# An attention backward pass: x^T and g^T of block 2 from staged tiles by TensorE, block 1 started tile by tile, K^T in five buffers ordered six steps ahead, dV in four

## Chip, cores and metric

One core of one Trainium2 chip. The metric is the device time of one launch in microseconds (us), the median of several executions.

## The reference

Two independent attention blocks (A, here "block 1", and B, "block 2") with a key and value cache, outputs concatenated, and the gradient of everything:

```python
# per block: B=8, Sq=96, D=640, H=32, Sk=512, Dh=128, bf16
def block(x, k_cache, v_cache, wq, wo):
    q = (x @ wq).reshape(B, Sq, H, Dh).transpose(0, 2, 1, 3)
    scores = einsum("bhqd,bhkd->bhqk", q, k_cache) * Dh ** -0.5
    p = softmax(scores)
    o = einsum("bhqk,bhkd->bhqd", p, v_cache)
    return o.transpose(0, 2, 1, 3).reshape(B, Sq, H * Dh) @ wo

out   = concatenate([block(A...), block(B...)], axis=-1)
grads = vjp(out, all ten inputs)(grad_out)      # returned with out: 11 outputs
```

## The kernel before

Work is put into steps ("ticks"): every piece is added with a step and a slot in it, and at the end all pieces are emitted sorted by step and slot. One step is one (head, batch) pair, 3.1 us at the steady pace; heads go in pairs (HP = 2), so K, V, K^T, V^T, dK, dV move once for two steps. All DMAs are issued by one engine's queue (SP) in the order in which they are added (`sp(...)` chains them). The parts that matter here, cut (`...`):

```python
OFF = dict(kt=-1, vt=2, vn=1, kn=4, dv=7, dk=10, s2=3, s3=3, s4=4, s5=5, s6=6, s7=8, s8=9)   # steps after the pair's own
HP = 2
HK = [   # head 0 and head 1 of a pair: steps of its projections (p..) and of its weight gradients (q..)
    dict(pA=-10, pB=-7, pC0=[-6, -4], pC1=[-5, -3], pD1=-2, pD0=0, qA0=21, qA1=25, qB=[28, 25]),
    dict(pA=-7, pB=-2, pC0=[-1, 1], pC1=[0, 2], pD1=3, pD0=6, qA0=29, qA1=33, qB=[36, 33], qD=[...]),
]

    def setup_T(which_, c):                        # x^T or g^T, column chunk c
        def f():
            ...
            if not first:                          # block 2: a transposing DMA from DRAM
                sp(nc.sync.dma_start_transpose(S[key][:, c, :], src_flat[:, c * 128:(c + 1) * 128]))
                return
            pt = bank([128, TT * 128], BF16, "tp_ps")
            for t in range(TT):                    # block 1: TensorE, six tiles of 128 tokens
                nc.tensor.transpose(pt[:, t * 128:(t + 1) * 128], S["x_nat" if which_ == 0 else "g_nat"][:, t, ...], ident[:])
            evac("act" if c % 2 == 0 else "dve", S[key][:, c, :], pt[:])
        return f

    if first:
        em.add(tick0 - 14, SL_LOAD, setup_nat(0))  # all of x, then all of g, 960 KB each
        em.add(tick0 - 14, SL_LOAD, setup_nat(1))
        ...
    else:
        for i in range(2 * DC):                    # ten transposing DMAs, 13 to 7 steps before block 2 begins
            em.add(tick0 - 13 + (2 * i) // 3, SL_LOAD + 0.5, setup_T(i // DC, i % DC))
        em.add(tick0 + 22, SL_LOAD + 0.5, setup_nat(1))
        em.add(tick0 + 25, SL_LOAD + 0.5, setup_nat(0))

    def p_ldT(h, b, which):                        # K^T or V^T of a pair of heads
            t_ = kvp.tile([128, F4 * KC, 16], BF16, name=key + "_p", bufs=4)
            sp(nc.sync.dma_start_transpose(t_[:], src))
    def c_s4(h, b):                                # dV of one (head, batch)
            ...
            if j == 0:
                st["dV_p"] = wk.tile([128, HP, KC * 128], BF16, name="dV_sb", bufs=3)
            nc.scalar.activation(dV_p[:, j], dV_ps[:], ACT.Identity, scale=1.0)
    def qB(h, di):                                 # dwo of one head, in two pieces (512 and 128 columns)
            if "dwo_sb" not in st:
                st["dwo_sb"] = hd.tile([128, D], BF16, name="dwo_sb", bufs=1)
            ...
            evac(EV["qB%d" % di], dwo_sb[:, c0:c0 + w], w_ps[:])       # ACT
    ...
            for di in range(len(dsplits)):
                em.add(c0t + hk["qB"][di], SL_HEAD + 1, qB(h, di))
            em.add(c0t + max(hk["qB"]) + 2, SL_LOAD + 0.3, qB_st(h))   # the store of dwo
```

Of the kernel before, what the change touches and what calls it, by code (L numbers as in the profile page):

```python
# [15 lines left out]
class Emitter:  # L16
# [24 lines left out]
SL_GRP = 95  # L41
SL_SETUP = 96

OFF = dict(kt=-1, vt=2, vn=1, kn=4, dv=7, dk=10, s2=3, s3=3, s4=4, s5=5, s6=6, s7=8, s8=9)
HP = 2
HK = [
    dict(pA=-10, pB=-7, pC0=[-6, -4], pC1=[-5, -3], pD1=-2, pD0=0, qA0=21, qA1=25, qB=[28, 25]),
    dict(pA=-7, pB=-2, pC0=[-1, 1], pC1=[0, 2], pD1=3, pD0=6, qA0=29, qA1=33, qB=[36, 33], qD=[(37, 0, 2), (38, 2, 4), (39, 4, 5)]),
]
EV = dict(pB0="act", pB1="dve", pC00="act", pC01="act", pC10="act", pC11="dve", pD0="dve", pD1="dve", qA0="dve", qA1="dve", qB0="act", qB1="act", qD="dve", gU="act")  # L50
GSPREAD0 = 9
PRIO_OFF = 2000
# [19 lines left out]
def build_block(tc, em, tick0, blk, x, kc, vc, wq, wo, g_all, out_all, dx, dk, dv, dwq, dwo, ident, ones, pools, HG=4, first=True, groups=None):  # L72
# [42 lines left out]
    S = {}  # L115
# [3 lines left out]

    sp = pools["sp"]  # L120

    def setup_T(which_, c):
        def f():
            key = "xT" if which_ == 0 else "gT"
            if c == 0:
                S[key] = const.tile([128, DC, T], BF16, name=key, bufs=1)
            src_flat = x_flat if which_ == 0 else g_flat
            if not first:
                sp(nc.sync.dma_start_transpose(S[key][:, c, :], src_flat[:, c * 128:(c + 1) * 128]))
                return  # L130
            pt = bank([128, TT * 128], BF16, "tp_ps")
            for t in range(TT):
                nc.tensor.transpose(pt[:, t * 128:(t + 1) * 128], S["x_nat" if which_ == 0 else "g_nat"][:, t, c * 128:(c + 1) * 128], ident[:])
            evac("act" if c % 2 == 0 else "dve", S[key][:, c, :], pt[:])
        return f

    def setup_nat(which_):
        def f():
            key = "x_nat" if which_ == 0 else "g_nat"
            src_flat = x_flat if which_ == 0 else g_flat  # L140
            t_ = const.tile([128, TT, D], BF16, name=key, bufs=1)
            sp(nc.sync.dma_start(t_[:], src_flat.rearrange("(t p) d -> p t d", p=128)))
            S[key] = t_
        return f

    def setup_acc():
# [11 lines left out]
                nc.vector.tensor_scalar(dst, src, float(sc), None, op0=ALU.mult)  # L158

    if first:  # L160
        em.add(tick0 - 14, SL_LOAD, setup_nat(0))
        em.add(tick0 - 14, SL_LOAD, setup_nat(1))
        for c in range(DC):
            em.add(tick0 - 9, SL_SETUP, setup_T(0, c))
            em.add(tick0 - 8, SL_SETUP, setup_T(1, c))
    else:
        for i in range(2 * DC):
            em.add(tick0 - 13 + (2 * i) // 3, SL_LOAD + 0.5, setup_T(i // DC, i % DC))
        em.add(tick0 + 22, SL_LOAD + 0.5, setup_nat(1))
        em.add(tick0 + 25, SL_LOAD + 0.5, setup_nat(0))  # L170

    def pA(h):
        def f():
            g, hh = h // HG, h % HG
            if hh == 0:
                G[g] = dict(wo_r=grp.tile([128, HG, D], BF16, name="wo_r", bufs=2))
            wo_h = G[g]["wo_r"][:, hh]
            sp(nc.sync.dma_start(wo_h, wo[h * 128:(h + 1) * 128, :]))
            j = h % HP
            if j == 0:  # L180
                wq_p = hd.tile([128, DC, HP * 128], BF16, name="wq_p", bufs=2)
                with nc.allow_non_contiguous_dma(reason="per-pair wq slice"):
                    sp(nc.sync.dma_start(wq_p[:], wq_v[:, :, h * 128:(h + HP) * 128]))
            else:
                wq_p = HS[(blk, h - j)]["wq_p"]
            HS[(blk, h)] = dict(wo_h=wo_h, wq_p=wq_p, wq_h=wq_p[:, :, j * 128:(j + 1) * 128])
        return f

    def pB(h):
        def f():  # L190
            st = HS[(blk, h)]
            woT_ps = bank([128, DC * 128], BF16, "woT_ps")
            for c in range(DC):
                nc.tensor.transpose(woT_ps[:, c * 128:(c + 1) * 128], st["wo_h"][:, c * 128:(c + 1) * 128], ident[:])
            woT_h = hd.tile([128, DC * 128], BF16, name="woT_h", bufs=1)
            evac(EV["pB0"], woT_h[:], woT_ps[:])
            st["woT_h"] = woT_h
            wqT_ps = bank([128, DC * 128], BF16, "wqT_ps")
            for c in range(DC):
                nc.tensor.transpose(wqT_ps[:, c * 128:(c + 1) * 128], st["wq_h"][:, c, :], ident[:])  # L200
            wqT_h = hst.tile([128, D], BF16, name="wqT_h")
            evac(EV["pB1"], wqT_h[:], wqT_ps[:])
            st["wqT_h"] = wqT_h
            st["QT_h"] = hd.tile([128, T], BF16, name="QT_h", bufs=4)
            st["dOT_h"] = hd.tile([128, T], BF16, name="dOT_h", bufs=4)
        return f

    def pC(h, which, si):
        def f():
            st = HS[(blk, h)]  # L210
            (t0, w) = tsplits[si]
            if which == 0:
                dst = st["QT_h"]
                lhs = lambda c: st["wq_h"][:, c, :]
                rhsT = S["xT"]
                sc = scale
            else:
                dst = st["dOT_h"]
                lhs = lambda c: st["woT_h"][:, c * 128:(c + 1) * 128]
                rhsT = S["gT"]  # L220
                sc = None
            q_ps = bank([128, w], F32, "q_ps")
            for c in range(DC):
                nc.tensor.matmul(q_ps[:], lhs(c), rhsT[:, c, t0:t0 + w], start=(c == 0), stop=(c == DC - 1))  # L224
            evac(EV["pC%d%d" % (which, si)], dst[:, t0:t0 + w], q_ps[:], sc)
        return f
# [19 lines left out]
    def p_ldT(h, b, which):  # L246
        def f():
            key = "KT" if which == 0 else "VT"
            t_ = kvp.tile([128, F4 * KC, 16], BF16, name=key + "_p", bufs=4)
            src = (kc if which == 0 else vc)[b, h:h + HP].rearrange("h (r f) d -> (h r) (f d)", r=R8)  # L250
            sp(nc.sync.dma_start_transpose(t_[:], src))
            for j in range(HP):
                half = t_[:, :, j * R8:(j + 1) * R8]
                CS.setdefault((blk, h + j, b), {})[key] = half.rearrange("p (f c) r -> p f c r", c=KC)
        return f
# [38 lines left out]
    def c_s2b(h, b):  # L294
        def f():
            with tc.high_priority(PRIO_OFF):
                st = CS[(blk, h, b)]
                E_sb = wk.tile([Sq, Sk], BF16, name="E_sb", bufs=2)
                rowsum = wk.tile([Sq, 1], F32, name="rowsum", bufs=3)
                nc.scalar.activation(E_sb[:].rearrange("q (a f) -> q a f", f=F4), st["S_ps"][:].rearrange("q (f a) -> q a f", f=F4), ACT.Exp, bias=st["negm"][:], scale=1.0, accum_out=rowsum[:])  # L300
                st["E_sb"], st["rowsum"] = E_sb, rowsum
                del st["S_ps"]
        return f
# [19 lines left out]
    def c_s45(k5, k4, k6):  # L323
        def f():
# [17 lines left out]
                    nc.tensor.transpose(PT_ps[:, c * Sq:(c + 1) * Sq], P_sb[:, c * 128:(c + 1) * 128], ident[0:Sq, 0:Sq])  # L342
            if ot_view is not None:
                OT_ps, hs, tok = ot_view
                nc.vector.tensor_copy(hs["OT_h"][:, tok], OT_ps)  # L345
            if k4 is not None:
                PT_sb = wk.tile([128, KC * Sq], BF16, name="PT_sb", bufs=3)
                nc.scalar.activation(PT_sb[:], PT_ps, ACT.Identity, scale=1.0)  # L348
# [3 lines left out]
    def c_s4(h, b):  # L352
        def f():
            st = CS[(blk, h, b)]
            hs = HS[(blk, h)]
            P_sb = st["P_sb"]
            dV_ps = bank([128, KC * 128], F32, "dV_ps")
            for c in range(KC):
                nc.tensor.matmul(dV_ps[:, c * 128:(c + 1) * 128], P_sb[:, c * 128:(c + 1) * 128], hs["dOnat_h"][:, b * 128:(b + 1) * 128], start=True, stop=True)  # L359
            j = h % HP  # L360
            if j == 0:
                st["dV_p"] = wk.tile([128, HP, KC * 128], BF16, name="dV_sb", bufs=3)
            dV_p = CS[(blk, h - j, b)]["dV_p"]
            nc.scalar.activation(dV_p[:, j], dV_ps[:], ACT.Identity, scale=1.0)  # L364
        return f
# [164 lines left out]
    for g in range(NG):  # L530
        h0 = GH0[g]
        for hh in range(groups[g]):
            h = h0 + hh
            j = h % HP
            c0t = tick0 + (h - j) * B
            hk = HK[j]
            em.add(c0t + (hk["pA"] if h > 0 or not first else -15), SL_LOAD, pA(h))
            em.add(c0t + hk["pB"], SL_HEAD, pB(h))
            em.add(c0t + OFF["s5"], SL_LOAD, h_alloc(h))
            for si in range(NTS):  # L540
# [4 lines left out]
            for b in range(B):  # L545
                ct = c0t + b * HP + j
                if j == 0:
                    em.add(ct + OFF["kt"], SLOTS["LOAD"], p_ldT(h, b, 0))
                    em.add(ct + OFF["vt"], SLOTS["LOAD"], p_ldT(h, b, 1))
                    em.add(ct + OFF["vn"], SLOTS["LOAD"] + 0.1, p_ldn(h, b, 1))  # L550
                    em.add(ct + OFF["kn"], SLOTS["LOAD"] + 0.1, p_ldn(h, b, 0))
                    em.add(ct + OFF["dv"], SLOTS["LOAD"] + 0.2, p_st(h, b, 1))
                    em.add(ct + OFF["dk"], SLOTS["LOAD"] + 0.2, p_st(h, b, 0))
# [156 lines left out]
```

## Time and profile before

| | kernel before |
|---|---|
| time, median of 3 (range) | 1689.2 us (1685.68 to 1693.71) |
| profiled execution | 1677.57 us, its span 1675.8 us, mean clock 0.995 |
| PE idle in the whole span (sum of gaps between matmuls) | 63.4 us |
| four heads at the steady pace (32 S matmuls) | 100.0 us |

The profiled execution of before is a quick one: 10 us under its median. How to read the stretches: cut where every 32nd S matmul begins (four heads of work); a group that takes 100 us runs at PE's own pace, and what it takes beyond 100 is lost somewhere.

### The profile page before, as it was taken

How to read it: one execution, taken by the hardware profiler on the slowest of the kernel's cores; microseconds unless marked ns; L12 is line 12 of the kernel's file. 1: busy time of each engine (PE TensorE's matmuls, PEld its weight loads, DVE VectorE, ACT ScalarE, POOL GpSimd, SP SyncE). 2: the span in 40 equal slices, each digit the busy share in tenths (PEclk: the TensorE clock that was granted, in tenths of full speed). 3: DMA queues.
4: the chain of work that ended last, by engine and by line, in shares of the span. 5: the costliest groups of instructions: out<-in, count | busy, mean ns of one | idle time of the engine just before them, and what ended most of it. 6: DMA issues, size and time to landing. Idle time of an engine off the chain costs nothing.

```text
span 1675.8 us, 55270 instructions
## 1 busy us (share of the span) xinstructions
PE 1609.0 (96%) x20670; PEld 1263.1 (75%) x20860; DVE 1363.4 (81%) x3381; ACT 1334.4 (80%) x3511; POOL 535.2 (32%) x1030
## 2 busy tenths in 40 slices
PE   6999999999999999999799999999999999999998
PEld 5777777777777777777577777777787777777776
DVE  4876788888888888888588778888888888888886
ACT  6988877878787797887677789788787877878783
POOL 2333333333333232332233323333233333333231
PEclk9999999999999999999899999999999999999999
DMA  8999999999999999999999999999999999999996
GB/s 242 265 272 262 258 275 292 267 287 271 277 281 269 264 294 287 272 280 256 262 297 288 270 290 286 278 292 277 295 267 270 275 286 278 271 276 259 277 277 192
DMA packets 378381, 458.11 MB, mean 273 GB/s; under 512 B 44288, under 2 KB 369920, under 8 KB 369920
## 3 DMA queue, kind: packets, MB, share of 16 engines
q1 hardware_dynamic: 378112, 454.57, 103.0%
q8 instruction: 163, 2.67, 0.7%
q14 instruction: 106, 0.87, 0.1%
HBM read 159.12 MB, written 159.12 MB: 190 GB/s over the span
## 4 chain that ended last, share of the span: by engine, by line
PE 73%; ACT 8%; DMA 8%; DVE 6%; issue 4%; SPq 1%; POOL 0%; ACTq 0%; DVEq 0%; POOLq 0%
PE q_ps L224 11%; PE o_ps L508 10%; PE dwo_ps L463 6%; PE dwq_ps L483 5%; PE S_ps L288 5%; PE dV_ps L359 5%; PE dP_ps L383 5%; PE dK_ps L425 5%; PE optp_ps L335 4%; PE optp_ps L342 4%; PE dq_dst_ps L409 4%; PE dq_dst_ps L402 4%; DMA out_dram<-dV_sb 3%; PE n_ps L239 3%; ACT E_sb L300 3%
## 5 line engine op out<-in xcount | busy, mean ns | idle before, releaser
L319 POOL TENSOR_SCALAR P_sb<-E_sb,rinv 96x512 bf16<-96x512 bf16 x512 | 353.9, 691 | 328.8 <-DVE rinv L310 327.9
L430 ACT ACTIVATE dK_sb<-dK_ps 128x512 bf16<-128x512 f32 x512 | 304.9, 595 | 168.7 <-PE dK_ps L425 158.8
L373 POOL TENSOR_TENSOR prod<-OT_h,dOT_h 128x96 bf16<-128x96 bf16 x512 | 187.4, 366 | 780.7 <-DVE OT_h L345 764.5
L387 DVE SCALAR_TENSOR_TENSOR dS_sb<-dP_ps,dl_ps,P_sb 96x512 bf16<-96x512 f32 x512 | 382.2, 746 | 28.4 <-PE dl_ps L385 17.5
L300 ACT ACTIVATE E_sb<-S_ps,negm 96x512 bf16<-96x512 f32 x512 | 349.7, 683 | 69.7 <-DVE negm L290 64.3
L290 DVE TENSOR_REDUCE negm<-S_ps 96x1 f32<-96x512 f32 x512 | 347.2, 678 | 57.9 <-PE S_ps L288 57.1
L364 ACT ACTIVATE dV_sb<-dV_ps 128x512 bf16<-128x512 f32 x512 | 309.6, 605 | 34.9 <-DMA out_dram<-dV_sb 23.9
L348 ACT ACTIVATE PT_sb<-optp_ps 128x384 bf16<-128x384 bf16 x512 | 253.5, 495 | 0.7 <-PE optp_ps L342 0.5
L411 DVE COPY dST_sb<-dq_dst_ps 128x384 bf16<-128x384 bf16 x512 | 177.8, 347 | 35.9 <-PE dq_dst_ps L409 30.9
L288 PE MATMUL S_ps<-KT_p,QT_h 128*96 128x512 bf16 x512 | 194.2, 379 | 8.6 <-DMA KT_p<-in_A_k_cache_dram 4.3
L425 PE MATMUL dK_ps<-Qnat_h,dS_sb 96*128 96x128 bf16 x2048 | 198.6, 220 | 0.0
L359 PE MATMUL dV_ps<-dOnat_h,P_sb 96*128 96x128 bf16 x2048 | 198.5, 219 | 0.2 <-ACT dV_sb L364 0.2
L383 PE MATMUL dP_ps<-VT_p,dOT_h 128*96 128x512 bf16 x512 | 195.5, 382 | 1.2 <-DMA VT_p<-in_B_v_cache_dram 0.9
L335 PE MATMUL optp_ps<-PT_sb,V_sb 128*128 128x96 bf16 x2048 | 172.4, 206 | 10.5 <-ACT PT_sb L348 5.4
L402 PEld LDWEIGHTS <-K_sb 128*128 128x128 bf16 x2048 | 133.6, 98 | 56.5 <-issue 7.0
L342 PE MATMUL optp_ps<-ident,P_sb 96*128 96x96 bf16 x2048 | 172.1, 205 | 3.7 <-POOL P_sb L319 3.7
L409 PE MATMUL dq_dst_ps<-ident,dS_sb 96*128 96x96 bf16 x2048 | 172.5, 206 | 0.0
L402 PE MATMUL dq_dst_ps<-dST_sb,K_sb 128*128 128x96 bf16 x2048 | 171.3, 206 | 0.0
L345 DVE CAST OT_h<-optp_ps 128x96 bf16<-128x96 f32 x512 | 126.4, 247 | 32.8 <-PE optp_ps L342 30.1
L508 PE MATMUL o_ps<-wo_r,OT_h 128*128 128x128 bf16 (+1 forms) x721 | 144.3, 294 | 2.5
L508 PE MATMUL o_ps<-wqT_h,dQT_h 128*128 128x128 bf16 (+1 forms) x721 | 144.2, 294 | 2.5
L224 PE MATMUL q_ps<-gT,woT_h 128*128 128x512 bf16 (+1 forms) x624 | 135.0, 324 | 8.5 <-DMA gT<-in_grad_out_dram 7.3
(66 smaller groups left out, 3019.4 us busy)
## 6 DMA issues: line engine op xcount, KB each, us to landing
out_dram<-dV_sb SPq DMA_DIRECT2D x256, 256.0 KB, 4.7
out_dram<-dK_sb SPq DMA_DIRECT2D x256, 256.0 KB, 4.7
V_sb<-in_A_v_cache_dram SPq DMA_DIRECT2D x128, 256.0 KB, 4.7
K_sb<-in_A_k_cache_dram SPq DMA_DIRECT2D x128, 256.0 KB, 4.5
V_sb<-in_B_v_cache_dram SPq DMA_DIRECT2D x128, 256.0 KB, 4.6
K_sb<-in_B_k_cache_dram SPq DMA_DIRECT2D x128, 256.0 KB, 4.5
out_dram<-dwo_sb SPq DMA_DIRECT2D x64, 160.0 KB, 4.6
out_dram<-dwq_sb SPq DMA_DIRECT2D x32, 320.0 KB, 4.7
```

The costliest lines, as they stand in the source:

```text
L224: nc.tensor.matmul(q_ps[:], lhs(c), rhsT[:, c, t0:t0 + w], start=(c == 0), stop=(c == DC - 1))
L290: nc.vector.tensor_reduce(negm[:], S_ps[:], axis=AX.X, op=ALU.max, negate=True)
L300: nc.scalar.activation(E_sb[:].rearrange("q (a f) -> q a f", f=F4), st["S_ps"][:].rearrange("q (f a) -> q a f", f=F4), ACT.Exp, bias=st["n ...
L319: nc.gpsimd.tensor_scalar(P_sb[:], st["E_sb"][:], st["rinv"][:], 0.0, op0=ALU.mult, op1=ALU.add)
L359: nc.tensor.matmul(dV_ps[:, c * 128:(c + 1) * 128], P_sb[:, c * 128:(c + 1) * 128], hs["dOnat_h"][:, b * 128:(b + 1) * 128], start=True, s ...
L364: nc.scalar.activation(dV_p[:, j], dV_ps[:], ACT.Identity, scale=1.0)
L383: nc.tensor.matmul(dP_ps[:], hs["dOT_h"][:, tok], st["VT"], start=True, stop=True)
L387: nc.vector.scalar_tensor_tensor(dS_sb[:].rearrange("q (a f) -> q a f", f=F4), dP_ps[:].rearrange("q (f a) -> q a f", f=F4), dl_ps[:, 0:1] ...
L402: nc.tensor.matmul(dQT_ps, st["K_sb"][:, c, :], st["dST_sb"][:, c * Sq:(c + 1) * Sq], start=(c == 0), stop=(c == KC - 1))
L425: nc.tensor.matmul(dK_ps[:, c * 128:(c + 1) * 128], dS_sb[:, c * 128:(c + 1) * 128], hs["Qnat_h"][:, b * 128:(b + 1) * 128], start=True, s ...
L430: nc.scalar.activation(dK_p[:, j], dK_ps[:], ACT.Identity, scale=1.0)
L508: nc.tensor.matmul(o_ps[:], src[:, t * 128:(t + 1) * 128], rhs, start=(hh == 0), stop=(hh == groups[g] - 1))
```

## The change

Intent: ten transposing DMAs at the crossing from block 1 to block 2 are replaced by twelve plain tile loads and 60 TensorE transposes; block 1 begins on single x tiles as they land; K^T is ordered two steps earlier with a fifth buffer, so that a late load does not stop PE; dV gets a fourth buffer, so that ACT does not wait for stores. Besides, g and x for block 2's weight gradients are loaded in twelve pieces instead of two, and therefore the first dwo work of block 2 moves later (`HK2`).

```diff
-OFF = dict(kt=-1, vt=2, vn=1, ...)
+OFF = dict(kt=-3, vt=2, vn=1, ...)
+HK1 = [dict(HK[0], pB=2, pC0=[-8, -6], pC1=[3, 3], pD1=3.5, pD0=6), dict(HK[1], pB=2, pC0=[-8, -6], pC1=[3, 3.6], pD1=4, pD0=7)]
+HK2 = [dict(HK[0], qA0=29, qB=[32, 31]), dict(HK[1], qA0=33)]
+GT0, ST0, ST1, NG0, NX0 = 2, -14, 7, 21, 26
...
+    def setup_stage(which_, t):                   # one tile of 128 tokens into a staging buffer
+            S[(key, t)] = wk.tile([128, D], BF16, name="ob", bufs=3)
+            sp(nc.sync.dma_start(S[(key, t)][:], src_flat[t * 128:(t + 1) * 128, :]))
-    def setup_T(which_, c):
+    def setup_T(which_, t):                       # five transposes of one tile, one evacuation
+            src = S[nat][:, t, :] if first else S.pop((nat, t))[:]
+            pt = bank([128, DC * 128], BF16, "tp_ps")
+            for c in range(DC):
+                nc.tensor.transpose(pt[:, c * 128:(c + 1) * 128], src[:, c * 128:(c + 1) * 128], ident[:])
...
     if first:
-        em.add(tick0 - 14, SL_LOAD, setup_nat(0))
-        em.add(tick0 - 14, SL_LOAD, setup_nat(1))
+        for t in range(TT):                       # x tile by tile, g later
+            em.add(tick0 - 15, SL_LOAD + (2 if late else 0), setup_nat(0, t, t + 1))
+            em.add(tick0 - (7 if late else 9), SL_HEAD, setup_T(0, t))
+            em.add(tick0 + GT0, SL_LOAD - 2, setup_nat(1, t, t + 1))
+            em.add(tick0 + GT0, SL_HEAD + (2 if late else -1), setup_T(1, t))
     else:
-        for i in range(2 * DC):
-            em.add(tick0 - 13 + (2 * i) // 3, SL_LOAD + 0.5, setup_T(i // DC, i % DC))
-        em.add(tick0 + 22, SL_LOAD + 0.5, setup_nat(1))
-        em.add(tick0 + 25, SL_LOAD + 0.5, setup_nat(0))
+        for i in range(2 * TT):
+            em.add(tick0 + ST0 + (ST1 * i) // (2 * TT), SL_LOAD + 0.5, setup_stage(i // TT, i % TT))
+            em.add(tick0 + ST0 + (ST1 * i) // (2 * TT) + 2, SL_SETUP, setup_T(i // TT, i % TT))
+        for t in range(TT):
+            em.add(tick0 + NG0 + t, SL_LOAD + 0.5, setup_nat(1, t, t + 1))
+            em.add(tick0 + NX0 + (3 * t) // 2, SL_LOAD + 0.5, setup_nat(0, t, t + 1))
...
-            t_ = kvp.tile([128, F4 * KC, 16], BF16, name=key + "_p", bufs=4)
+            t_ = kvp.tile([128, F4 * KC, 16], BF16, name=key + "_p", bufs=5 if which == 0 else 4)
...
-                st["dV_p"] = wk.tile([128, HP, KC * 128], BF16, name="dV_sb", bufs=3)
+                st["dV_p"] = wk.tile([128, HP, KC * 128], BF16, name="dV_sb", bufs=4)
...
-            hk = HK[j]
+            hk = (HK if h >= HP else HK1 if first else HK2)[j]
```

Cut from the diff: the load of wq as a piece of its own, rowsum in two buffers instead of three, and a higher priority for the evacuation of O^T.

## The prediction

> **What bounds the kernel now.** I read the page first, then the stretches, the waits, the timeline of the queue that issues all DMAs, and raw DMA packet records.
>
> ```profile
> span 1675.8 us, 55270 instructions
> PE 1609.0 (96%) x20670; PEld 1263.1 (75%) x20860; DVE 1363.4 (81%) x3381; ACT 1334.4 (80%) x3511; POOL 535.2 (32%) x1030
> ...
> q1 hardware_dynamic: 378112, 454.57, 103.0%
> ```
>
> PE looks like the bound, but the DMA engines are as full: packet time equals 103% of 16 engines' span. The stretches say where PE loses. I cut at every 32nd S matmul (four heads; here rounded) after finding their times in the timeline.
>
> ```profile
> core 0: us, PE busy (x) PEld busy (x) DVE busy (x) ACT busy (x) POOL busy (x), PEclk, DMA share, GB/s
> 0.00:20.00 20.00, 11.59 (x121) 9.34 (x124) 4.41 (x10) 9.11 (x13) 0.70 (x6) 1.00 0.92 250
> 20.00:105.00 85.00, 74.99 (x1010) 58.86 (x1014) 67.68 (x171) 75.27 (x199) 31.92 (x61) 1.00 1.01 260
> 105.00:210.00 105.00, 101.49 (x1286) 78.78 (x1297) 77.81 (x189) 88.94 (x238) 33.32 (x64) 1.00 1.04 261
> ...
> 717.00:833.00 116.00, 102.95 (x1285) 80.27 (x1296) 85.56 (x213) 82.11 (x215) 32.93 (x63) 0.94 1.03 259
> 833.00:939.00 106.00, 101.96 (x1291) 79.88 (x1301) 86.12 (x215) 81.79 (x217) 33.54 (x65) 0.98 1.06 288
> ...
> 1041.00:1541.00 500.00, 494.58 (x6439) 390.85 (x6498) 429.11 (x1070) 409.08 (x1081) 166.80 (x320) 1.00 1.05 278
> ```
>
> The row from 1041 to 1541 is five groups of four heads at 100 us each, 1 us of PE idle per group: PE's own pace. Against 100, the group that crosses from block 1 to block 2 (717 to 833) loses 16, the next one 6, the one from 105 to 210 about 5, the others of block 1 together some 6. The first 105 us lose 18.4 us of idle PE (20 less 11.59, 85 less 74.99).
>
> ```profile
> PE tp_ps L133 <- DMA x_nat<-in_A_x_dram: 8.0, 1, 8.0
> PE q_ps L224 <- DMA gT<-in_grad_out_dram: 7.3, 2, 5.3
> ...
> ACT dV_sb L364 <- DMA out_dram<-dV_sb: 23.9, 24, 2.6
> ```
>
> The big waits are all for DMAs: x at the start, g^T at the crossing, the buffers of dV (ACT's wait, which reaches PE only when ACT falls behind). Now the issuing queue at the crossing:
>
> ```profile
> 783.36 4.21 SPq L129 DMA_TRANSPOSE xT<-in_B_x_dram  x2
> 787.67 1.46 SPq L251 DMA_TRANSPOSE VT_p<-in_A_v_cache_dram  x1
> 789.18 0.58 SPq L178 DMA_DIRECT2D wo_r<-in_B_wo_dram  x1
> 789.80 0.43 SPq L183 DMA_DIRECT2D wq_p<-in_B_wq_dram  x1
> ...
> 793.53 1.56 SPq L251 DMA_TRANSPOSE KT_p<-in_A_k_cache_dram  x1
> ...
> 796.27 3.53 SPq L129 DMA_TRANSPOSE gT<-in_grad_out_dram  x2
> ```
>
> Each row starts where the one before ends. I checked this for the whole run: the 1766 DMA issues take 1490.6 us and the gaps between them 162 us (median 46 ns); from 28 us to 1642 us no gap exceeds 0.45 us. Nor is the queue waiting for buffers: when a K^T load is issued, the last reader of the buffer it overwrites has been done for 8 to 18 us (means of eight loads in a row, after the first eight). So the DMA stream runs without rest at nearly PE's pace. From the end of a K^T issue to its use there are only 6 to 12 us on average, 3 to 4 us at the narrowest, and the load itself takes 5.2 us to land. That is the reading on which I choose the number: **PE and the DMA stream are co-bounds**, and before 939 us it is the stream that sets the pace.
>
> **What the Trainium skill says.** "Perfetto Trace Analysis", section "What DMA-bound means", names a sequencer track that is solid DMA slices as one form of DMA-bound, and notes that such a slice is descriptor generation, not movement. The trace agrees on the solid track. "VectorE: DVE Perf Modes", section "The three transpose paths", gives 390 ns for a 128x128 transpose on TensorE and 1309 ns by DMA. Here the 30 g transposes take 1.84 us together, 61 ns each when queued, and an x^T transposing DMA (six such blocks) occupies the issuing queue 1.3 us or more. "Advanced Engine Details and Errata", section "X-Bar Transpose (TRN2)", calls transposing DMAs as fast as regular ones. The packets disagree for x^T and g^T: 256-byte packets of 34.9 ns against 61.3 ns for 1280-byte ones, 2.8 times the time per byte. "TensorE: Matmul & The Clock Gate", Part 1, says the clock halves after an idle window of about 3.4 us; PEclk is 0.68 in 800 to 820 us, around the 5.29 us wait for g^T.
>
> **The change part by part.**
>
> *Crossing.* Ten transposing DMAs go: 16.15 us of the issuing queue and 7680 packets x 34.9 ns / 16 engines = 16.7 us of all engines. Twelve tile loads of 160 KB come: 12 x (0.53 + 0.09) = 7.4 us of queue and 12 x 128 packets x 61.3 ns / 16 = 5.9 us of engines. Net 9 us of queue, 11 us of engine time. Six K^T steps there took 53.2 us (770.43 to 823.59) for a usual 37.5, so 15.7 extra; with the new loads I expect 6 or 7 extra. PE gets 60 transposes x 61 ns = 3.7 us, and ACT and DVE six evacuations each (ACT 0.8, DVE 0.56 by the rows of x^T before), which have room at 80%. Since PE waited 12 us there, its 3.7 us lie mostly in what would be waiting. Gain: 16 less about 6, so **10**, of which some 1.5 is the restored clock.
>
> *x and g of block 2 for the weight gradients* are loaded in twelve pieces over ticks 21 to 33, not as two of 960 KB. The bytes are the same, and the stretch 833 to 939 already moves 288 GB/s, the most of any; the K^T issue just behind g_nat took 4.72 us. Spreading removes such clumps, the load stays: **2** of the 6.
>
> *Start.* Four x tiles, then wq, then the rest; PE can begin near 3.5 us (an estimate: a 160 KB load lands in 3 to 4 us, first issue 0.74) instead of 8.0. Q^T comes before g, so the first S moves from 21.4 to about 12. But K^T for the 17th pair step is issued at 99 and used at 105: by then the DMA stream paces. What the stream gains is its one real rest, 3.8 us from 24.4 to 28.2, where the first dV store waited for dV, and somewhat fuller engines (0.76 of their time in 20 to 30 us). Gain **5**, not the 9 that PE's idle time suggests.
>
> *dV in four buffers* removes most of ACT's 23.9 us; of the PE stalls only those behind ACT gain (1.46 us at 71.8, about 1 us each at 518, 925, 944). *K^T two ticks earlier and a fifth buffer*: in an unbroken stream this only moves K^T ahead of other loads. V is next in need, with about the same margin (6.4 us, lands in 4.7), so PE's 15.5 us of K^T waits (4.3 on PE, 11.2 on its weight loads, overlapping) shrink by little before V takes their place. Together **3**.
>
> *Rest.* OT_h first on DVE, rowsum in two (E_sb has two already), the later first dwo of block 2: 0. The tail after the last S (1638.9) is untouched.
>
> Sum: 10 + 2 + 5 + 3 = 20, and the rate after 1041 is PE's own. I take 2 off again for new order waits (second rival): 18 of 1676, 1.1%.
>
> **Rivals.**
>
> *PE is the only bound.* Then nearly all excess is there to be had: start 9 to 11, crossing 11, the stretch behind it 4, K^T and dV waits 6: 30 to 35 us, about 1656. For it: PE 96%, flat 100 us groups. Against it: the unbroken queue and the 3 to 4 us minimum margins.
>
> *The staged tiles block the queue.* They have three buffers, tiles are ordered 7/12 tick apart and transposed two ticks later, so the fourth load waits for PE's first transposes; a waiting load holds up K^T and V behind it. With a tick of 3.1 us this could cost 3 to 6 us at the crossing, most of the gain: about 1675. For it: the queue trails PE's order by about a tick already. Against: K^T's two extra ticks cover it.
>
> *Only PE's wait moves.* Loads that start earlier find full engines and land later; V or wo becomes the wait in place of K^T and g^T: gain under 8, 1682 or more.
>
> **Range and chances.** 1689.2 - 18 x (1689.2 / 1675.8) = 1671; I lean towards the first rival by a quarter of the difference and say **1667**. The range 1654 to 1681 spans from the first rival to the third. Faster by 2% needs below 1655.4, nearly all of the first rival: 0.15. Slower needs a blocked queue all along: 0.03. Within 2%: 0.82.
>
> **What would show it.** Right: L133 with 120 transposes, no L129; first S near 12 us; no rest of the queue near 25 us; the group across the crossing near 106 and PEclk 1.0 there; dV waits under 5 us; the issuing queue still solid; the five late groups still 100. Wrong if the first 105 us shorten by 9 or more, or groups of block 1 all fall to 100 (then PE alone was the bound), or if the queue shows waits at L133's tiles (then the second rival).

## More of the kernel before

Runs were made on more than one chip, and the same kernel differs between chips by more than most effects studied here; so times are compared only within one set, a set being kernels that ran on the same chip together with the kernel before.

## The result, and the profile after

| | before | after |
|---|---|---|
| median (range, runs) | 1687.79 us (1685.68 to 1693.71, 4) | 1670.28 us (1666.86 to 1672.68, 4) |
| profiled span, clock | 1675.8 us, 0.995 | 1668.0 us, 0.993 |
| PE idle in the span | 63.4 us | 47.5 us |

The ratio is 0.9889, 95% interval 0.9858 to 0.9921: within 2%. Here and below a ratio is the mean time of one kernel's runs over the mean of the other's of the same rounds, so not quite the ratio of the medians quoted. The gain is 17.5 us by the medians. The changed kernel was run again in two later sets on chip 5: 13.5 us (ratio 0.9942) and 17.1 us (0.9889) below the kernel before.

The page after, first line, engines and the DMA queue:

```profile
span 1668.0 us, 55517 instructions
PE 1616.8 (97%) x20920; PEld 1265.7 (76%) x20920; DVE 1368.3 (82%) x3389; ACT 1339.2 (80%) x3517; POOL 533.5 (32%) x1030
...
q1 hardware_dynamic: 372160, 454.57, 102.7%
```

Both bounds are as full as they were: the DMA engines moved the same 454.57 MB in 5952 fewer packets, and their share went from 103.0% to 102.7%.

The stretches after, cut at its own 32nd S matmuls (columns: stretch, length, busy time and count of PE, weight loads, DVE, ACT and POOL; the last three are clock, DMA share and GB/s):

```profile
0.00:20.00 20.00, 13.07 (x114) 8.74 (x115) 5.14 (x12) 9.60 (x16) 1.20 (x7) 1.00 0.88 224
20.00:105.00 85.00, 77.72 (x1049) 62.45 (x1047) 69.01 (x173) 75.23 (x198) 32.06 (x62) 0.96 1.03 272
...
708.00:819.00 111.00, 105.69 (x1365) 83.00 (x1364) 88.81 (x223) 86.69 (x226) 33.60 (x65) 0.98 1.02 263
819.00:927.00 108.00, 101.91 (x1301) 79.30 (x1300) 86.17 (x215) 82.45 (x216) 33.22 (x65) 0.98 1.05 288
927.00:1038.00 111.00, 100.75 (x1299) 79.29 (x1298) 78.07 (x189) 89.56 (x239) 33.13 (x64) 0.95 1.03 274
1041.00:1541.00 500.00, 498.02 (x6518) 391.33 (x6516) 430.59 (x1072) 410.75 (x1084) 167.07 (x322) 1.00 1.05 279
```

The row 927 to 1038 is the surprise: 10 us of idle PE and a clock of 0.95 in a group which in the kernel before took 101.9 us. The row 20 to 105 has a clock of 0.96, where the kernel before had 1.00. From the starts of S matmuls 0, 32, 224, 256, 288, 320 and 480, the stages of both profiles:

| stage (S matmuls) | before | after | gain |
|---|---|---|---|
| start to 32 | 104.8 | 103.5 | 1.3 |
| 32 to 224, block 1 | 611.8 | 604.8 | 7.0 |
| 224 to 256, the crossing | 116.6 | 110.5 | 6.1 |
| 256 to 288 | 106.1 | 108.2 | -2.1 |
| 288 to 320 | 101.9 | 111.4 | -9.5 |
| 320 to 480 | 500.3 | 499.3 | 1.0 |
| 480 to the end | 134.3 | 130.3 | 4.0 |

The sum is 7.8 us, the difference of the spans; the 10 us more that the medians show cannot be laid to stages, because before was profiled in one quick run only. The 4.0 us of the last row belong to no term of the prediction, which held the end untouched. In before PE waits there for ACT (1.2, 0.7 and 0.3 us between 1547 and 1552 us), and after it does not; no run tells which part of the change removed that. One profile each is also little: the changed kernel was profiled three times, and its crossing took 110.5, 105.9 and 111.1 us.

The waits after (time in all, times, longest):

```profile
ACT dwo_sb L162 <- DMA out_dram<-dwo_sb: 13.9, 5, 10.1
...
PE optp_ps L350 <- ACT dwo_sb L162: 9.8, 1, 9.8
...
PE woT_ps L209 <- DMA wo_r<-in_A_wo_dram: 4.8, 4, 2.2
...
PE optp_ps L350 <- DMA V_sb<-in_B_v_cache_dram: 4.2, 2, 2.6
...
PE tp_ps L151 <- DMA ob<-in_grad_out_dram: 3.3, 2, 2.8
```

The waits for g^T, for K^T and for the buffers of dV are gone from the top. In their place stands one wait of ACT for the store of dwo, 10.1 us long, and PE's wait for ACT, 9.8 us. In place of g^T PE waits for the staged tiles (3.3 us for g, 1.8 for x), and in place of K^T for wo (4.8 us in four places, 0.3 before) and for V (4.2 us in two). V was predicted; wo stands only in the third rival. In the group of dV's evacuations (busy us, mean ns | idle before, releaser; the row before ended "34.9 <-DMA out_dram<-dV_sb 23.9") nothing is left:

```profile
L380 ACT ACTIVATE dV_sb<-dV_ps 128x512 bf16<-128x512 f32 x512 | 309.7, 605 | 0.3 <-PE dV_ps L375 0.3
```

The timeline of the stall (start, duration; in brackets the idle time ahead of it and its releaser), ACT and the issuing queue:

```profile
927.25 0.49 ACT L364 ACTIVATE PT_sb<-optp_ps 128x384 bf16<-128x384 bf16 x1
937.79 0.28 ACT L162 ACTIVATE dwo_sb<-dwo_ps 128x128 bf16<-128x128 f32 x1 [10.05 <-DMA out_dram<-dwo_sb]
```

```profile
933.31 0.46 SPq L485 DMA_DIRECT2D out_dram<-dwo_sb  x1
```

ACT stands from 927.74 to 937.79 before the 128-column piece of head 1's dwo. It may overwrite the one `dwo_sb` only when head 0's dwo has been stored, and that store is issued at 933.31, and ACT goes on 4.5 us later. The steps say why. `HK2` puts head 0's pieces at steps 32 and 31, so its store, two steps after the later of its two pieces, comes at step 34; head 1's first piece stays at step 33. Before, the store was at step 30. A wait of one instruction stops everything behind it on its engine: the Trainium skill, "Perfetto Trace Analysis", section "Per-instruction lifecycle: what the profiler-reported window actually captures", calls ACT, DVE and GPSIMD strict FIFOs, and the trace agrees, for the 0.59 us evacuation of dV behind it starts only at 937.96.

The stall costs more than PE's 9.8 us of waiting. PE goes on at 938.12, and the clock stays low for some time after:

```profile
938.00:941.20 3.20, 3.08 (x27) 2.64 (x27) 1.78 (x5) 2.69 (x8) 1.03 (x2) 0.50 1.07 351
```

It is 0.50 from 931.0 to 941.2 us. A matmul of dP, 0.38 us long just before the stall, takes 0.63 us in that row. Half of the 3.1 us is 1.5 us (an estimate from the clock of 0.50); with the wait that is 11.3 of the 11.6 us by which this group exceeds 99.8.

The crossing in the issuing queue (a row with x2 is two issues in a row, from the start of the first to the end of the second):

```profile
771.49 4.69 SPq L140 DMA_DIRECT2D ob<-in_B_x_dram  x2
776.23 1.10 SPq L266 DMA_TRANSPOSE KT_p<-in_A_k_cache_dram  x1
777.39 0.57 SPq L277 DMA_DIRECT2D V_sb<-in_A_v_cache_dram  x1
778.05 0.41 SPq L286 DMA_DIRECT2D out_dram<-dV_sb  x1
```

Two tile loads of some 0.4 us each span 4.69 us: between them the queue stood 3.94 us. The second issue starts at 775.84, as PE's transposes of an earlier tile end at 775.81, so it waited for a staging buffer; K^T, V and dV stood behind. The Trainium skill, "DMA: Bandwidth & Descriptors", section "Anatomy of one DMA — SWDGE (gpsimd) path", says that DMA engines do not wait on semaphores, a wait being served on the issuing sequencer before dispatch. The trace shows just that, on the path that SP uses. This is the second rival of the prediction. In again_after the same wait took 5.13 us. What it costs in the time no run shows.

### The profile page after: what moved, and what is told of

Its sections match the earlier page's. It is cut to its first block, busy times and chain, and to the rows that moved or that the text cites. A ratio compares the mean times of both kernels' runs of the same rounds, so it can differ in the third digit from the quotient of the medians. Undisturbed runs are those within 1.5% of the kernel's fastest.

```text
span 1668.0 us, 55517 instructions
## 1 busy us (share of the span) xinstructions
PE 1616.8 (97%) x20920; PEld 1265.7 (76%) x20920; DVE 1368.3 (82%) x3389; ACT 1339.2 (80%) x3517; POOL 533.5 (32%) x1030
## 3 DMA queue, kind: packets, MB, share of 16 engines
q1 hardware_dynamic: 372160, 454.57, 102.7%
## 4 chain that ended last, share of the span: by engine, by line
PE 79%; ACT 6%; DMA 6%; DVE 5%; issue 2%; SPq 1%; POOL 0%; ACTq 0%; DVEq 0%
PE q_ps L239 11%; PE o_ps L524 10%; PE dwo_ps L479 6%; PE dV_ps L375 5%; PE dP_ps L399 5%; PE dwq_ps L499 5%; PE S_ps L303 5%; PE dK_ps L441 5%; PE optp_ps L350 4%; PE optp_ps L357 4%; PE dq_dst_ps L418 4%; PE dq_dst_ps L425 4%; PE n_ps L254 3%; PE nat_ps L465 2%; DVE negm L305 2%
## 5 line engine op out<-in xcount | busy, mean ns | idle before, releaser
L350 PE MATMUL optp_ps<-PT_sb,V_sb 128*128 128x96 bf16 x2048 | 172.4, 206 | 18.7 <-ACT dwo_sb L162 9.8
L524 PE MATMUL o_ps<-wo_r,OT_h 128*128 128x512 bf16 (+1 forms) x768 | 149.3, 299 | 0.0
L524 PE MATMUL o_ps<-wqT_h,dQT_h 128*128 128x512 bf16 (+1 forms) x768 | 148.5, 299 | 0.0
L350 PEld LDWEIGHTS <-V_sb 128*128 128x128 bf16 x2048 | 125.2, 97 | 23.0 <-issue 18.2
```

Source lines behind the costliest of these rows:

```text
L350: nc.tensor.matmul(OT_ps, st["V_sb"][:, c, :], st["PT_sb"][:, c * Sq:(c + 1) * Sq], start=(c == 0), stop=(c == KC - 1))
L524: nc.tensor.matmul(o_ps[:], src[:, t * 128:(t + 1) * 128], rhs, start=(hh == 0), stop=(hh == groups[g] - 1))
```

## The experiments

Twelve runs, three sets. Time before on the same chip in the same set: 1683.22 us in the first (1670.34 to 1690.88, 11 runs, chip 5), 1665.55 in the second (1658.78 to 1669.52, 11 runs, chip 15), 1687.79 in the third (1679.79 to 1698.83, 11 runs, chip 5 again). On chip 15 the kernel before is about 20 us faster. In the set of chip 15 the changed kernel was not run, and the kernel before was not profiled. Groups of four heads are quoted from the profiles as three numbers: 224 to 256 (the crossing), 256 to 288, and 288 to 320.

| run | chip | median (range) | ratio to before [95%] | groups |
|---|---|---|---|---|
| again_after | 5 | 1669.72 (1667.38 to 1675.84) | 0.9942 [0.9905, 0.9979] | 105.9, 109.6, 112.1 |
| e_qb | 5 | 1658.67 (1656.47 to 1668.63) | 0.9879 [0.9842, 0.9916] | 106.8, 106.5, 104.5 |
| u_xt | 5 | 1676.24 (1673.11 to 1688.28) | 0.9983 [0.9945, 1.0022] | 115.6, 106.7, 112.1 |
| u_kt | 5 | 1668.26 (1660.01 to 1672.44) | 0.9918 [0.9882, 0.9955] | 107.0, 108.6, 110.3 |
| u_dv | 15 | 1661.31 (1659.02 to 1666.77) | 0.9985 [0.9963, 1.0007] | 107.3, 109.8, 108.0 |
| u_start | 15 | 1662.88 (1659.21 to 1667.64) | 0.9991 [0.9968, 1.0014] | 106.2, 107.6, 111.9 |
| b_nost | 15 | 1646.83 (1645.43 to 1649.19) | 0.9895 [0.9876, 0.9915] | 109.7, 102.7, 100.2 |
| e_nost | 15 | 1639.90 (1638.82 to 1641.98) | 0.9855 [0.9831, 0.9878] | 106.7, 101.3, 101.1 |
| after_3 | 5 | 1670.65 (1664.35 to 1673.89) | 0.9889 [0.9852, 0.9926] | 111.1, 105.6, 111.8 |
| e_dwo2 | 5 | 1665.94 (1661.51 to 1669.32) | 0.9865 [0.9829, 0.9901] | 109.3, 108.8, 100.4 |
| e_best | 5 | 1692.16 (1687.28 to 1699.90) | 1.0033 [0.9990, 1.0075] | 109.4, 110.1, 103.5 |
| u_nat | 5 | 1658.03 (1656.17 to 1661.50) | 0.9824 [0.9789, 0.9859] | 109.2, 106.3, 101.0 |

All gave the right result but b_nost and e_nost. One build more failed before any run: two `dwo_sb` beside five K^T buffers did not fit into memory (10 KB per partition wanted, 8.75 KB left).

### again_after: the mark

No edit: the changed kernel again, as the mark of the first set.

> The changed kernel once more, as the mark for the three others on the same chip. Ratio to the kernel before 0.986 to 0.992; the 9.8 us stall of PE behind the dwo eviction near 928 us is there again.

1669.72 us, and the stall of dwo is back at 925.6 us with 9.48 us: it belongs to the kernel, not to one run. The ratio, 0.9942, missed the expected 0.986 to 0.992: in this set the change gained less.

### e_qb: head 1's dwo moved behind head 0's store

Theory: the stall is worth what PE idles in it. Rival: the DMA stream, given no pause by the stall, takes the time elsewhere.

```diff
-HK2 = [dict(HK[0], qA0=29, qB=[32, 31]), dict(HK[1], qA0=33)]
+HK2 = [dict(HK[0], qA0=29, qB=[31, 30]), dict(HK[1], qA0=33, qB=[36, 36])]
```

> Only the first pair of block 2 differs: the first head's dwo pieces one step earlier (31, 30) and both of the second head's pieces at 36, so that the eviction no longer comes before the store it waits for has landed. Theory (the stall of 9.8 us is a cost that the change brought and DMAs don't hide): 7 to 10 us less than the changed kernel, 0.4 to 0.6%, and the group of four heads from S 288 to S 320 back at 100 to 102 us. Rival (PE and the DMA stream are co-bounds throughout, so the stall is given back by loads that come late): under 3 us less, and new DMA waits of PE after 930 us.

1658.67 us, 11 less than the mark. The group from S 288 to S 320 of e_qb, where the stall was:

```profile
921.10:1025.60 104.50, 101.95 (x1307) 79.59 (x1306) 78.45 (x191) 90.28 (x243) 33.34 (x64) 0.98 1.07 294
```

PE idles 2.6 us in 104.5, and the stream carries 294 GB/s, more than in any stretch quoted so far. The group did not come down to the expected 100 to 102: PE waits 1.5 us for ACT's dK and 0.6 us for V^T near 927. PE's idle time in the whole span falls from 46.7 us to 37.4. The theory holds, and the gain is more than the 7 to 10 us expected: a stall of one instruction on ACT, in one place, took 11 us of the change's gain, about what its wait and the low clock after it add up to.

### u_xt: x^T and g^T of block 2 by transposing DMAs again

Theory: this part is the largest of the gain. Rival: what the transposing DMAs cost was hidden, and little changes.

```diff
-        for i in range(2 * TT):
-            em.add(... setup_stage(i // TT, i % TT))
-            em.add(... setup_T(i // TT, i % TT))
+        for i in range(2 * DC):
+            em.add(tick0 - 13 + (2 * i) // 3, SL_LOAD + 0.5, setup_Tdma(i // DC, i % DC))
```

> The changed kernel with x^T and g^T of block 2 by ten transposing DMAs again, the rest as changed. Theory (the crossing was the largest gain, some 6 us in the two profiles): 5 to 10 us more than the changed kernel, the waits of PE for g^T back at 5 us or more. Rival (K^T ordered earlier already covers the crossing, the new PE transposes and waits for staged tiles cost as much as they save): within 2 us of the changed kernel.

1676.24 us, 6.5 more than the mark (7.1 by the spans). The crossing takes 115.6 us again, for 105.9, and its wait is back:

```profile
PE q_ps L246 <- DMA gT<-in_grad_out_dram: 9.8, 3, 5.4
```

The time says 6.5 us, the span 7.1. By the group the crossing is worth 9.7 us against this mark, but 5.1 and 4.5 against the other two profiles of the changed kernel (110.5 and 111.1). The clock takes part in that: it is 0.96 in the crossing of u_xt, 1.00 in again_after and 0.98 and 0.97 in the other two.

### u_kt: K^T as before

Theory (the prediction's): in a stream without rest an earlier order only exchanges one load for another, and this part is worth nothing. Rival: K^T's waits were true stops, and each that goes is won.

```diff
-OFF = dict(kt=-3, ...)
+OFF = dict(kt=-1, ...)
-            t_ = kvp.tile(..., bufs=5 if which == 0 else 4)
+            t_ = kvp.tile(..., bufs=4)
```

> The changed kernel with K^T in four buffers and ordered at the old place. My prediction held this to be worth little, since in an unbroken stream of DMAs another load takes its place: 0 to 2 us more than the changed kernel. Rival (K^T was the tightest load, its margin rose from 7 to 13 us while V's stayed near 7.5): 4 to 8 us more, with PE's waits for K^T back at 5 us or more.

1668.26 us, 1.5 less than the mark, which is within the spread of both. In this kernel the part buys nothing, as predicted. Waits for K^T came back, 3.3 us of PE and 5.9 us of its weight loads, without a longer time.

### u_dv: dV in three buffers

Theory: ACT's waits for dV stores reach PE and cost time. Rival: they lie beside PE's work and cost nothing.

```diff
-                st["dV_p"] = wk.tile(..., name="dV_sb", bufs=4)
+                st["dV_p"] = wk.tile(..., name="dV_sb", bufs=3)
```

> The changed kernel with dV in three buffers again. Theory (ACT's waits for dV's stores, 23.9 us before and none after, reached PE only where ACT ran late): 2 to 5 us more than the changed kernel (some 1670 us in the last set), the waits of ACT for dV's stores back at 15 us or more, and the group from S 32 to S 64 back above 103 us. Rival (the waits were all beside PE's work): within 1 us, no group longer.

1661.31 us on chip 15; the changed kernel was not in this set, so the size of the part stays open. The waits are back:

```profile
ACT dV_sb L380 <- DMA out_dram<-dV_sb: 13.8, 14, 3.0
```

They are a little under the expected 15 us. Block 1 from S 32 to 224 took 602.5 us, against 602 to 607 in the profiles with four buffers (without e_nost, e_dwo2 and e_best; most of them on another chip), and the group from S 32 to 64 took 100.6, not above 103. That speaks for the rival. But behind ACT's two waits of 2.95 and 2.55 us near 900 PE waited 1.7 and 0.8 us, so a part does reach PE, as the theory said. The three groups add up to 325.1 us against 327.6 in again_after, which the shorter stall of dwo explains: 6.0 us here instead of 9.5; why it was shorter was not looked into.

### u_start: block 1 begins as before

Theory: the start is worth 5 us. Rival: S 32 waits for the stream, and most of an earlier start is lost by then.

```diff
-        for t in range(TT): ...                    # x tile by tile, g at step 2
+        em.add(tick0 - 14, SL_LOAD, setup_nat_all(0))
+        em.add(tick0 - 14, SL_LOAD, setup_nat_all(1))
+        for c in range(DC): ...                    # transposes by column chunk, as before
-            hk = (HK if h >= HP else HK1 if first else HK2)[j]
+            hk = (HK if h >= HP or first else HK2)[j]
```

Cut: the first loads of wq, wo and K^T and the buffer of wo^T are put back too.

> The changed kernel with block 1's start as before: x and g whole, their transposes by columns, Q and dO together. Theory (the DMA stream paces by 100 us, so an earlier first S is mostly lost): first S at 21, S 32 at 104 to 106, 2 to 5 us more than the changed kernel. Rival (PE's earlier start is kept): S 32 at 108 or later, 6 us or more in the time.

The first S is at 24.1 us instead of 16.7 (u_dv, same chip), S 32 at 107.5 instead of 102.7, S 224 at 711.1 instead of 705.2. The median, 1662.88, is only 1.6 us above u_dv's, with ranges that overlap. The 4.8 us at S 32 are no measure of the start either: in the ten profiles that have the new start and all stores S 32 comes between 101.2 and 107.1 us, and in the kernel before it came at 104.8. The expectation missed both at the first S (21) and at S 32 (104 to 106). What the start is worth is not shown.

### b_nost and e_nost: half of the dK stores left out

Theory: PE and the DMA stream are co-bounds; with 16.8 MB of stores per block gone, half of dK, the stretches of block 1 fall to PE's pace. Rival: PE alone is the bound, and nothing moves. b_nost is the kernel before with this edit, e_nost is e_qb with it. The result is wrong (two outputs are not written in full).

```diff
         def f():
+            if which == 0 and b % 2 == 1:
+                return
             t_ = CS[(blk, h, b)]["dV_p" if which == 1 else "dK_p"]
```

> The kernel before with every other dK store left out (a wrong result on purpose): 128 of 1766 DMAs and 7% of the bytes fewer, PE's work the same. Theory (the DMA stream is a co-bound, and its lateness is what PE loses between 60 and 940 us outside the crossing): 12 to 25 us less than the kernel before, groups of block 1 at 100 us, and the issuing queue with gaps. Rival (PE alone): under 4 us less.

> The mended version (dwo of block 2's first pair moved) with every other dK store left out, a wrong result on purpose. Theory (co-bound): there is little lateness left except near 75, at the crossing and from 819 to 940; those shrink and the time falls by 8 to 15 us from 1658. Rival (PE alone is the bound now): under 4 us.

b_nost took 1646.83 us, 18.7 less than before on the same chip. That is within the 12 to 25 us expected. The stretch from 105 to 717 us, first of the kernel before (profiled in an earlier set, with a median near chip 5's), then of b_nost (chip 15):

```profile
105.00:717.00 612.00, 598.98 (x7731) 470.54 (x7802) 507.64 (x1261) 499.55 (x1321) 200.72 (x386) 1.00 1.06 276
```

```profile
105.00:717.00 612.00, 609.71 (x7967) 479.68 (x7965) 518.52 (x1288) 509.68 (x1351) 204.79 (x394) 1.00 1.04 260
```

With 260 GB/s to move instead of 276, PE idles 2.3 us in 612 instead of 13.0, and the 192 S matmuls there take 599.9 us instead of 611.8. ACT's waits for dV stores, which the edit does not touch, are 3.7 us instead of 23.9 (u_dv, with all stores and three buffers on chip 15, had 13.8). The time, compared on one chip, shows that the kernel before hangs on the DMA stream: PE's work is the same and 18.7 us go. That most of it lay in block 1 is read from two profiles that may differ by the chip as well. The crossing still takes 109.7 us, with 7.5 us of waits for g^T: these do not come from the bytes left out. e_nost took 1639.90 us; its groups of block 1 are 599.2 us for six. It comes out some 19 us under e_qb, more than expected, but on another chip, so that difference is not a measured gain. Within the set, b_nost to e_nost is 6.9 us: that is what the change and its repair are worth with the stream relieved. With all stores they were not run on this chip, so whether this is less than usual there is open.

### after_3: the mark of the third set

No edit.

> The changed kernel as the mark of this set. The kernel before moved between chips (1683 and 1666 us median), and I hold that the speed of its DMA stream did; the changed kernel should move less: 1660 to 1672 us. The stall behind the dwo store near 925 us: 6 to 10 us.

1670.65 us, stall 9.57 us, both as expected.

### e_dwo2: two dwo buffers instead of another order

Theory: the stall goes, and is worth what it was in e_qb. Room for the buffer was made by K^T as before, which u_kt had shown to cost nothing.

```diff
-                st["dwo_sb"] = hd.tile([128, D], BF16, name="dwo_sb", bufs=1)
+                st["dwo_sb"] = hd.tile([128, D], BF16, name="dwo_sb", bufs=2)
-OFF = dict(kt=-3, ...)  and K^T bufs=5
+OFF = dict(kt=-1, ...)  and K^T bufs=4
```

> The changed kernel, K^T in four buffers at its old place again, and the memory given to a second buffer of dwo. Theory (K^T's fifth buffer is worth nothing, the wait for dwo's store is worth its 9 us): 8 to 12 us less than the changed kernel, no wait for dwo's stores. Rival (both the fifth buffer and the early order matter once the stall is gone): 3 us or less.

1665.94 us, 4.7 less than the mark, half of what was expected. The stall is gone (group 100.4), but block 1 took 609.3 us where u_kt took 603.2, and it shows more waits than u_kt's. The K^T waits of block 1 in the two kernels, u_kt first:

```profile
PEld L303 <- DMA KT_p<-in_A_k_cache_dram: 3.1, 4, 1.0
```

```profile
PEld L303 <- DMA KT_p<-in_A_k_cache_dram: 11.9, 11, 2.1
```

These are of the weight loads; PE's own waits for K^T in block 1 are 1.2 us in u_kt and 2.9 us here. The order of all loads in block 1 is the same in both kernels. So "K^T earlier is worth nothing" is not safe: in this kernel its lack may cost the missing 3 to 7 us. This stays open.

### e_best: all together, and V a step earlier

Meant as the best version: e_dwo2 with e_qb's order, and V ordered one step earlier, since V had become the tightest load.

```diff
-OFF = dict(kt=-3, vt=2, vn=1, ...)
+OFF = dict(kt=-1, vt=2, vn=0, ...)
+  dwo_sb bufs=2, K^T bufs=4, HK2 as in e_qb
```

> As the run with two dwo buffers, with block 2's first dwo pieces spread as in the mended version and V ordered one step earlier, since PE's last DMA waits behind the crossing are for V. Theory: 1 to 4 us less than with two dwo buffers alone, V waits near 905 us gone. Rival (the stream is merely late there, so wo or K^T takes V's place): within 1 us.

1692.16 us, 21.5 more than the mark: the expectation failed altogether. The even stretch of block 2 in again_after, then in e_best:

```profile
1141.00:1441.00 300.00, 298.72 (x3902) 234.47 (x3901) 258.34 (x643) 245.92 (x649) 99.80 (x192) 1.00 1.06 283
```

```profile
1141.00:1441.00 300.00, 292.73 (x3805) 228.82 (x3802) 252.26 (x626) 238.33 (x629) 96.66 (x186) 0.99 1.02 274
```

PE idles 7.3 us in 300 instead of 1.3, and the DMA share is lower, 1.02 for 1.06, and so is the rate: the stream carries less and PE waits more. The waits of e_best:

```profile
ACT dK_sb L446 <- DMA out_dram<-dK_sb: 31.9, 25, 3.4
PEld L303 <- DMA KT_p<-in_A_k_cache_dram: 18.5, 19, 1.8
```

PE itself waits 18.0 us in 14 places for ACT's evacuations of dK, and 8.8 us for K^T. V one step earlier falls into the same step as V^T and K, so two steps of the queue are now "K^T, dV" and "V^T, K, V, dK", where they were "K^T, V, dV" and "V^T, K, dK". The bytes are equal, the alternation is lost, and K^T comes out behind a lump. That the order is the cause is argued from this one run; K^T's late order and the two dwo buffers are in it too, though e_dwo2 has both without the harm.

### u_nat: the two whole loads and dwo's old steps again

Theory: the spread loads are worth next to nothing and cost the stall through `HK2`, so that without both the time falls. Rival: the lumps of two 960 KB loads cost what the stall cost.

```diff
-        for t in range(TT):                        # twelve pieces, steps 21 to 33
-            em.add(tick0 + NG0 + t, ..., setup_nat(1, t, t + 1))
-            em.add(tick0 + NX0 + (3 * t) // 2, ..., setup_nat(0, t, t + 1))
+        em.add(tick0 + 22, SL_LOAD + 0.5, setup_nat_all(1))
+        em.add(tick0 + 25, SL_LOAD + 0.5, setup_nat_all(0))
-            hk = (HK if h >= HP else HK1 if first else HK2)[j]
+            hk = (HK if h >= HP else HK1 if first else HK)[j]
```

> The changed kernel with g and x of block 2 for the weight gradients as two whole loads at the old place, and the first pair's dwo work at the old place, so without the dwo stall. My prediction gave the spreading 2 us. Theory (the stall cost 9 and the spreading saved 2): 5 to 8 us less than the changed kernel, the groups from S 256 to S 320 losing 8 to 12 us together against 100 each. Rival (the spreading saves as much as the stall costs): within 2 us of the changed kernel.

1658.03 us, 12.6 less than the mark, where 5 to 8 were expected, and the best ratio of all, 0.9824. The group 288 to 320 is 101.0 for 111.8, and 256 to 288 is 106.3 for 105.6 (109.6 in again_after): the whole loads cost nothing that the profiles show. Its interval reaches across 2%, so it cannot be called faster than before by more than that. Together with e_qb: the spreading is worth about nothing, the step that it forced on dwo costs 10 to 12 us.

## Why the prediction was right or wrong

**The total was right: 1667 predicted, 1670.28 measured; 18 us of gain by its sum (22 in the number 1667, which leans towards the first rival), 17.5 measured.** That PE and the DMA stream bound together was right as well: b_nost shows it by its time, and only by profiles that it is block 1 where the stream sets the pace. But one term of the sum was wrong by some 11 us, and the other parts together brought about as much more than was held. That the two cancel is luck.

*The crossing, 10 us.* Measured 6.5 (u_xt against again_after). The group gave 4.5 to 9.7, by the profile that is taken for the changed kernel, so the term was somewhat too large. In this profile the crossing was 110.5 us rather than "near 106", but it was 105.9 in again_after and 111.1 in after_3. Clock 0.98 for the expected 1.0.

*Loads of block 2, 2 us, and "the later first dwo of block 2: 0".* Here a step of the prediction failed. The second half has the sign wrong: the part costs 10 to 12 us (u_nat, e_qb). What the runs showed instead: ACT waited 10.1 us for the store of dwo and PE 9.8 us for ACT, and with the step put right (e_qb) the time fell by 11 us. The diff showed all of it: a single `dwo_sb`, a store two steps after the last piece, and head 1's first piece at step 33 with head 0's store at 34. I read `HK2` as "later", and did not follow its buffer.

*The start, 5 us.* Between the two profiles S 32 gained 1.3 us; in the time (u_start against u_dv) it is 1.6 with overlapping ranges. So it is not confirmed. The first S came at 17.3, not near 12, and of its 4.1 us most was gone by S 32: PE waited for wo (1.5 us at 16, 2.2 us at 77), and the clock was 0.96 for 1.00 from 20 to 105 (an estimate: 0.04 x 85 = 3.4 us of PE's time). The transposes of g run from 13.1 to 17.9 us in the trace, so S came among them and not ahead of them. The rest of the queue near 25 us is gone, as said.

*dV and K^T, 3 us.* dV's waits fell from 23.9 us to none; its size in the time stays open, and u_dv shows 2.5 us of PE's waits behind them. K^T gave nothing in u_kt, and V and wo took its place, but e_dwo2 leaves this in doubt.

*Two us off for order waits.* The staging buffers did stop the queue for 3.94 us, with K^T and V behind. By the prediction's own words a wait there meant the second rival; its total, about 1675, did not come. No run separates the cost.

**What was too small.** Without the stall, the change is worth 24.6 us (e_qb, 1683.22 less 1658.67) or 29.8 us (u_nat, 1687.79 less 1658.03) on chip 5, not 20. The undone parts do not add up to that: 6.5 for the crossing, 1.6 for the start, nothing measured for K^T, dV open. In a stream without slack one part may cover the waits that another would cover too, so undoing one alone shows less than its share. That is argued, not shown. So the rival "PE is the only bound", 30 to 35 us, had the better size for the repaired kernel on chip 5, and the wrong reason: b_nost gains 18.7 us where only bytes are removed.

**The other chip.** On chip 15 u_dv and u_start, the changed kernel with one part undone each, were 4.2 and 2.7 us below the kernel before, with intervals that reach 1. The changed kernel was not run there. Unless each of the two undone parts is worth some 10 us alone, the 17.5 us are a gain of chip 5 and not of every chip.

**Named signs that came out:** 120 tile transposes (30, 30 and 60) and no transposing DMA for x and g; no rest of the queue near 25 us (largest gap 0.96 us, at 39.7); dV waits under 5 us; the first 105 us shorter by 1.3, not by 9; the five late groups at 99.8 to 100.3. Missed: first S near 12 us. Half: waits of the queue at the staged tiles; the queue less solid than before (from 28 to 1630 us gaps up to 1.8 us beside those waits, against 0.45); and groups of block 1 that came down to 100.8 on average without all being 100.

## What to carry to other kernels

When a change moves work later, follow every buffer that the work writes and the store that frees it: one evacuation that waits on an in-order engine stopped PE for 9.8 us here, more than the largest part of the change had won. A stage read from one profile is a rough measure: three profiles of the same code gave 105.9 to 111.1 us for the crossing. Undoing parts one at a time need not sum to the whole, as here. A total that fits proves no term; the two repairs (e_qb, u_nat), each 11 to 13 us faster than the changed kernel, were found only because the stage table did not fit.

## What the Trainium skill lacked or had wrong

- "Advanced Engine Details and Errata", section "X-Bar Transpose (TRN2)", calls transposing DMAs as fast as regular ones. In the kernel before a 256-byte packet of x^T or g^T took 34.9 ns and a 1280-byte packet 61.3 ns, 2.8 times the time per byte; these packets are also the smaller ones, and no run separates size from transposing. Putting the ten transposing DMAs back cost 6.5 us (u_xt).
- "VectorE: DVE Perf Modes", section "The three transpose paths", gives 390 ns for a 128x128 transpose on TensorE. Queued back to back, 30 of them took 1.84 us in the kernel before, 61 ns each; the 219 ns that the trace gives for one tile's transpose is the duration of one, and they overlap.
- None has that the order of equal loads and stores in one queue can change what it carries, as one run suggests. e_best: 274 GB/s for 283 in the same stretch, and 21.5 us more in all.
- None has how far one kernel differs between chips. The kernel before took 1665.55 us on one and 1683.22 and 1687.79 on another, more than the change was worth.
